# Three weight chunks over GpSimd's queue behind a head's sums, and twenty extra matmuls in five slots

## The chip, the cores and the metric

The kernel runs on one core of a Trainium2 chip. The metric is the time of one execution on the device in microseconds (us); for the kernel before it is the median of three runs. The core's engines are named as in the profile: PE (TensorE, matrix products), DVE (VectorE), ACT (ScalarE), POOL (GpSimd) and SP (SyncE, which here only issues DMA transfers).

## The reference

Three stages follow each other: causal attention with a bias from cumulated `s`, 4 batches of 8 heads, 576 positions, 64 numbers per head; a layer with a clipped gate; a second layer with another gate. The weights `w_in` and `w_out` are float64.

```python
scores = scale * np.matmul(q, k.transpose(0, 1, 3, 2))
cum = np.cumsum(np.maximum(s, 0.0), axis=-1)
bias = -(cum[:, :, :, None] - cum[:, :, None, :])
scores = np.where(causal, -1000000000.0, scores + np.minimum(bias, 0.0))
attn = np.exp(scores - np.max(scores, axis=-1, keepdims=True))
attn = attn / (np.sum(attn, axis=-1, keepdims=True) + 1e-09)
x = np.matmul(attn, v)               # then (2304 tokens, 512)
h = x @ w_in                         # w_in 512 x 2048
x = (h * np.clip(h + 3.0, 0.0, 6.0) / 6.0) @ w_out
h = x @ w2_in
x = (h * (1.0 / (1.0 + np.exp(-h)))) @ w2_out
```

## The kernel before, in words

Attention works on heads of blocks. A block is one batch's first 256 queries (part A) or its other 320 (part B); the blocks come as A0 A1 A2 B0 A3 B1 B2 B3, with eight heads each. The first 22 heads are "whole": their products run in plain fp32. A head of part A goes through PE scores `ps0A`, `ps1A` (line L518), DVE masking into `pb0A`, `pb1A` (L540), ACT's exponential with row sums (L558), DVE's reciprocal of the sums (L567), PE transposes `pt0A` (L586), PE products with v into `poA` (L693), and DVE's scaling into `xtA` (L700), which PE transposes into `pxA` for each pair of heads (L711).

Layer 1 works on finished blocks, and its matmuls lie between those of the heads to come. A step takes one or two of 16 slices of the hidden layer for one block: 24 matmuls into `ph` (L266 to L268), the gate on ACT and DVE (`g`, L279, and `gl`, L286), and 24 matmuls into `acc` (L305 to L307), three for each product since numbers are split in a high and a low part. There is one `ph` bank, so a step's first matmul waits for the gate of the step before. A step of the first kind needs the `wi` and `wo` pieces of its slices.

The weights arrive as 32 chunks, `rawi_0`, `rawo_0`, `rawi_1` and so on, each a load of 512 KB (L147) of float64 words that are turned into two fp32 parts on the chip: ACT takes fields out of the words (L159, L160), POOL scales them (L162), DVE joins them (L178, L182), ACT rounds the high part (L120) and DVE takes the rest as the low part `wi` or `wo` (L193). A `Feed` hands these pieces out in ticks: a tick loads a chunk, takes the fields of the one three ticks before, joins that of four before, and rounds that of five before.

The work is written in slots. A slot scores head `cur`, transposes and multiplies head `p1` (the one before), finishes `p2`, asks for the loads of a head to come, may do a layer-1 step (`mm`), and runs the ticks `tk`. Nine slots have no step, 68 have one each. Three chunks load before slot 0. Slots 0 to 8 tick 0.4 times each, so three ticks fire there: `rawo_1` in slot 2 (`p1` is head 1), `rawi_2` in slot 5 (head 4) and `rawo_2` in slot 7 (head 6); from slot 9 on there are two ticks per slot. Slots without a step run three small bf16 matmuls, `keep_clock` (L86), into the unused `ph` bank. All loads go through SP's queue, where a whole head has four: q, k, v and two rows of cumulated biases, from `pairs` for the first four heads and from `pair_d` in DRAM for the others (L429).

The order of the written program isn't the final one: the kernel passes through a tile scheduler, which sets each engine's order from its own estimate of when things are ready. All engines and queues then work in order.

Of the kernel before, what the change touches and what calls it, by code (L numbers as in the profile page):

```python
# [11 lines left out]
I32 = mybir.dt.int32  # L12
# [5 lines left out]
P = 128  # L18
# [4 lines left out]
def f32(ap):  # L23
    return ap.bitcast(F32)
# [3 lines left out]
def kernel(  # L28
# [15 lines left out]
    nc = tc.nc  # L44

    B, H, D, S = qT.shape
# [36 lines left out]
    def keep_clock(n, beside):  # L83
        for _ in range(n):
            o = idle[:, : beside.shape[-1]]
            nc.tensor.matmul(o, busy[:, :P], beside, start=True, stop=True)  # L86

    def heads_of(x):
        return x.bitcast(BF16).rearrange("p (n two) -> p n two", two=2)[:, :, 1]
# [40 lines left out]
    class Chunk:  # L130
# [7 lines left out]
            pool, tag = self.home  # L138
            return pool.tile(shape, dt, tag=tag, name=f"{name}{self.nm}")

        def load(self):
            if self.src.dtype == F32:
                self.val = self.place([P, DM], F32, "raw")
                nc.sync.dma_start(self.val, self.src)
            else:
                raw = self.place([P, 2 * DM], I32, "raw")
                nc.sync.dma_start(raw, self.src.bitcast(I32))  # L147
                words = raw.rearrange("p (n two) -> p n two", two=2)
                self.words = words[:, :, 0], words[:, :, 1]

# [44 lines left out]
    class Feed:  # L195


        def __init__(self, keys, hi_eng, lo_eng):
            self.ch = [Chunk(*k) for k in keys]
            self.hi_eng, self.lo_eng = hi_eng, lo_eng  # L200
            self.t = 0

        def done(self):
            return self.t >= len(self.ch) + 3 + 2

        def tick(self):
            n = len(self.ch)
            t = self.t - 3
            lo = self.lo_eng[t % len(self.lo_eng)] if 0 <= t - 2 < n else ""
            if lo:  # L210
                self.ch[t - 2].high(self.hi_eng[t % len(self.hi_eng)])
            if 0 <= t < n:
                self.ch[t].fields()
            if lo == "p":
                self.ch[t - 2].low(lo)
            if 0 <= t - 1 < n:
                self.ch[t - 1].join()
            if lo == "v":
                self.ch[t - 2].low(lo)
            if self.t < n:  # L220
                self.ch[self.t].load()
            self.t += 1


# [112 lines left out]
    def bank(kind, shape, name):  # L337
        pool, tag = turns[kind][turn[kind] % len(turns[kind])]
        turn[kind] += 1
        return pool.tile(shape, F32, tag=tag, name=name)  # L340
# [35 lines left out]
    class Head:  # L376
# [3 lines left out]
        def __init__(self, b, part, h, whole, at):  # L380
            self.b, self.part, self.h, self.whole, self.at = b, part, h, whole, at
            self.slot = at % 2
            self.bh = b * H + h
            self.nm = f"{part}{b}_{h}"
            self.chunks = [c for c in range(NCH) if (CH[c][0] < T1) == (part == "A")]
            self.q0 = CH[self.chunks[0]][0]
            self.nk = CH[self.chunks[-1]][0] + CH[self.chunks[-1]][1]
            self.nq = self.nk - self.q0
            self.nkc = self.chunks[-1] + 1
            self.groups = [[0, 1]] if part == "A" else [[0, 1], [2, 3]]  # L390
            self.prob, self.PT, self.pt, self.pS, self.rest = {}, {}, {}, {}, []
            self.pieces = []
            self.odd = h % 2
            for c in self.chunks[:: -1 if self.odd and part == "B" else 1]:
                w = CH[c][0] + CH[c][1]
                self.pieces += [(c, 0, w, True)] if w <= 512 else [
                    (c, 0, w // 2, False), (c, w // 2, w, True)]
            self.full = [c for c in self.chunks if c < NFULL]
# [251 lines left out]
        def av(self):  # L650
# [31 lines left out]
            nc.scalar.copy(tmp[mine, :], po[other, :])  # L682
            self.rest = [(x[mine, :], po[mine, a:z], tmp[mine, a:z]) for x, a, z in outs]

        def av_whole(self):

            b, h, nq = self.b, self.h, self.nq
            n, nch = P, len(self.chunks)
            po = bank("o", [P, nch, D], f"po{self.nm}")
            for c in self.chunks:  # L690
                for kc in range(c + 1):
                    a = CH[c][0] - max(CH[kc][0], self.q0)
                    nc.tensor.matmul(  # L693
                        po[:, c, :], self.PT[kc][0][:, a : a + n], self.va[:, kc, :],
                        start=kc == 0, stop=kc == c,
                    )
            if h % 2 == 0:
                xt[b] = apool.tile([P, nch, 2 * D], F32, tag=f"xZ{h // 2 % 2 + 2}", name=f"xt{self.nm}")
            r = self.sums[:, : nch].rearrange("p (c o) -> p c o", o=1)
            nc.vector.tensor_tensor(  # L700
                out=xt[b][:, :, h % 2 * D :][:, :, :D], in0=po,
                in1=r.to_broadcast([P, nch, D]), op=ALU.mult,
            )
# [89 lines left out]
    def slot(cur, p1, p2, nx, loads, mm, tk=(0, 0, 0, 0)):  # L793

        nonlocal step
        ng = len(p1.groups) if p1 else 0
        npc = len(cur.pieces) if cur else 0

        def scores(i):
            if i < npc:  # L800
                cur.score(i)
                cur.soft(i)

        def exps(i):
            if i < npc:
                cur.expo(i)

        def transposed(i):
            if i < ng:
                p1.trans(i)  # L810
                p1.trans_low(i)

        scores(0)
        scores(1)
        exps(0)
        if p2:
            p2.av_sum()
        ticks(tk[0])
        if mm:
            first(step, 0)  # L820
        if p1:
            p1.v_high()
        exps(1)
        scores(2)
        if nx:
            nx.qk_high()
        transposed(0)
        if p1 and p1.part == "B" and p1.odd:
            p1.tail_parts(p1.raw[:, :NFULL, :], p1.raw[:TAIL, NFULL, :])
        if p1 and not mm:  # L830
            keep_clock(3, heads_of(p1.prob[1]))
        if p1:
            p1.v_low()
        exps(2)
        if cur:
            cur.load_v()
        if nx and npc <= 3:
            nx.qk_low()
        ticks(tk[1])
        if mm:  # L840
            first(step, 1)
            gate_high(step)
        scores(3)
        if nx and npc > 3:
            nx.qk_low()
        exps(3)
        for hd in loads:
            hd.load()
        transposed(1)
        if cur:  # L850
            cur.norm()
        ticks(tk[2])
        if mm:
            second(step - 1, 0)
        if mm:
            gate_low(step)
        if p1 and p1.part == "B" and not p1.odd:
            p1.tail(cur)
        ticks(tk[3])
        if nx:  # L860
            nx.places()
        for hd in loads:
            hd.load_cum()
        if mm:
            second(step - 1, 1)
        if p1:
            p1.av()
        if mm:
            step += 1
# [17 lines left out]
    for has_head, has_step in plan:  # L887
        cur = at(k) if has_head else None
        nx = at(k + 1) if has_head else None
        loads = []  # L890
        while has_head and loaded < len(heads) and loaded <= k + (
            2
        ):
            loads.append(heads[loaded])
            loaded += 1
        k += has_head and cur is not None
        tk = [0, 0, 0, 0]
        if not feed.done():
            rate = ((0.4,)*9+(2,))[min(nslot, len(((0.4,)*9+(2,))) - 1)]
            for i in range(4):  # L900
                feed_at += rate / 4
                tk[i] = int(feed_at)
                feed_at -= tk[i]
        slot(cur, p1, p2, nx, loads, has_step, tk)
        if nslot == 9:
            split_rows()
        p1, p2 = cur, p1
        nslot += 1
        if nslot == H + 1:
            p2.av_sum()  # L910
            p2 = None
            split1(0)
            turns["s"] = turns["s"][:1]
        if has_step and step in first_step[1:NB1]:
            blk = first_step.index(step)
            assert k - (cur is not None) >= (blk + 1) * H
            if p2:
                p2.av_sum()
                p2 = None
            if blk == NB1 - 1:  # L920
                cx.close()
                xpool = cx.enter_context(
                    tc.tile_pool(name="xlast", bufs=1, side="right", reuse_waits="tile")
                )
            split1(blk)
            if blk == NB1 - 1:
                break
# [364 lines left out]
```

## Time and profile before

| | |
|---|---|
| median of 3 runs | 996.71 us (996.62 to 997.44) |
| the profiled execution | 997.93 us |
| its span, first to last instruction | 996.1 us |
| mean granted clock of PE | 0.992 |
| busy: PE, DVE, ACT, POOL | 973.4, 737.3, 510.8, 266.4 us |
| transfers | 125.41 MB, 126 GB/s over the span |

The span is read in stretches of time, each with the busy time of every engine, the clock granted to PE (1.00 is 2.4 GHz, half of it 1.2 GHz) and the share of the DMA engines. An engine that is full in a stretch bounds it; where none is, the waits tell which engine waited for which. Timelines list instructions in order of start; matmuls overlap, so the pitch from start to start is what one costs, not its duration.

### The profile page before, as it was taken

How to read it: one execution, taken by the hardware profiler on the slowest of the kernel's cores; microseconds unless marked ns; L12 is line 12 of the kernel's file. 1: busy time of each engine (PE TensorE's matmuls, PEld its weight loads, DVE VectorE, ACT ScalarE, POOL GpSimd, SP SyncE). 2: the span in 40 equal slices, each digit the busy share in tenths (PEclk: the TensorE clock that was granted, in tenths of full speed). 3: DMA queues.
4: the chain of work that ended last, by engine and by line, in shares of the span. 5: the costliest groups of instructions: out<-in, count | busy, mean ns of one | idle time of the engine just before them, and what ended most of it. 6: DMA issues, size and time to landing. Idle time of an engine off the chain costs nothing.

```text
span 996.1 us, 17938 instructions
## 1 busy us (share of the span) xinstructions
PE 973.4 (98%) x6268; PEld 896.2 (90%) x6268; DVE 737.3 (74%) x1757; ACT 510.8 (51%) x1177; POOL 266.4 (27%) x323
## 2 busy tenths in 40 slices
PE   8998999999999999999999999999999999999997
PEld 5888999999999999999997877898988989889996
DVE  6899998888789888988866899779674434743343
ACT  6898645555455555555546566455443323432332
POOL 2122433343333443433425466425000000000000
PEclk9899999999999999999999999999999999999999
DMA  5885122312222223222215967434354233442421
GB/s 176 238 285 187 41 55 76 90 49 60 83 77 75 72 59 92 60 61 83 60 32 180 394 225 239 163 116 190 135 193 169 81 141 116 162 154 75 148 75 64
DMA packets 54419, 125.41 MB, mean 126 GB/s; under 512 B 12332, under 2 KB 34076, under 8 KB 51000
## 3 DMA queue, kind: packets, MB, share of 16 engines
q1 hardware_dynamic: 53880, 123.60, 37.7%
q8 instruction: 50, 0.82, 0.3%
q10 hardware_dynamic: 448, 0.66, 0.2%
q14 instruction: 41, 0.34, 0.1%
HBM read 99.52 MB, written 24.69 MB: 125 GB/s over the span
## 4 chain that ended last, share of the span: by engine, by line
PE 74%; DVE 12%; DMA 4%; issue 4%; POOL 3%; ACT 1%; SPq 1%; POOLq 0%; DVEq 0%; ACTq 0%
PE a L1089 6%; PE a L1090 6%; PE a L1091 6%; PE h L1072 5%; PE h L1074 5%; PE h L1073 5%; PE ph L266 5%; PE ph L267 4%; PE ph L268 4%; PE acc L306 4%; PE acc L305 4%; PE acc L307 4%; PE poB L678 3%; DMA rawi<-in_w2i_dram 2%; POOL rawi L167 2%
## 5 line engine op out<-in xcount | busy, mean ns | idle before, releaser
L266 PE MATMUL ph<-xh,wi 128*128 128x256 f32 (+1 forms) x512 | 153.7, 302 | 4.4 <-DVE g L279 4.2
L306 PE MATMUL acc<-gl,wo 128*128 128x256 f32 (+1 forms) x512 | 151.6, 298 | 1.6 <-DVE gl L286 1.6
L267 PE MATMUL ph<-xl,wi 128*128 128x256 f32 (+1 forms) x512 | 151.4, 296 | 0.0
L268 PE MATMUL ph<-xh,wi 128*128 128x256 f32 (+1 forms) x512 | 151.2, 295 | 0.0
L307 PE MATMUL acc<-gh,wo 128*128 128x256 f32 (+1 forms) x512 | 150.3, 295 | 0.0
L305 PE MATMUL acc<-gh,wo 128*128 128x256 f32 (+1 forms) x512 | 143.6, 297 | 0.0
L1131 ACT ACTIVATE gh<-h 128x384 fp32r<-128x384 f32 x96 | 50.3, 524 | 178.7 <-DVE h L1139 178.5
L1089 PE MATMUL a<-wo,gh 128*128 128x512 f32 x288 | 113.6, 395 | 1.5 <-ACT gh L1131 1.1
L1090 PE MATMUL a<-wo,gh 128*128 128x512 f32 x288 | 113.1, 393 | 0.0
L266 PEld LDWEIGHTS ph<-xh,wi 128*128 128x128 f32 x512 | 96.9, 189 | 9.6 <-PE acc L307 1.9
L306 PEld LDWEIGHTS acc<-gl,wo 128*128 128x128 f32 x512 | 96.6, 189 | 5.7 <-DVE gl L286 2.7
L267 PEld LDWEIGHTS ph<-xl,wi 128*128 128x128 f32 x512 | 97.1, 190 | 3.1
L268 PEld LDWEIGHTS ph<-xh,wi 128*128 128x128 f32 x512 | 96.9, 189 | 3.0
L307 PEld LDWEIGHTS acc<-gh,wo 128*128 128x128 f32 x512 | 96.6, 189 | 3.3
L305 PEld LDWEIGHTS acc<-gh,wo 128*128 128x128 f32 x512 | 95.4, 188 | 3.5 <-DVE gh L122 0.2
L1091 PE MATMUL a<-wo,gl 128*128 128x512 f32 x288 | 90.5, 393 | 0.0
L1133 DVE TENSOR_TENSOR gl<-h,gh 128x384 fp32r<-128x384 f32 x96 | 53.4, 556 | 40.4 <-ACT h L1132 38.8
L114 POOL TENSOR_SCALAR gh<-g 128x512 fp32r<-128x512 f32 x68 | 50.0, 738 | 102.7 <-DVE g L279 88.2
L1139 DVE TENSOR_TENSOR h<-h,u 128x384 f32<-128x384 f32 x72 | 40.0, 556 | 49.8 <-PE h L1074 49.4
L1072 PE MATMUL h<-x0t,w 128*128 128x384 f32 x192 | 65.0, 339 | 0.7 <-DVE u L1139 0.7
L1073 PE MATMUL h<-x1t,w 128*128 128x384 f32 x192 | 65.0, 338 | 0.0
L1074 PE MATMUL h<-x0t,w 128*128 128x384 f32 x192 | 64.8, 338 | 0.0
(222 smaller groups left out, 2526.6 us busy)
## 6 DMA issues: line engine op xcount, KB each, us to landing
w<-w_d SPq DMA_DIRECT2D x18, 1792.0 KB
w_d<-w SPq DMA_DIRECT2D x8, 1792.0 KB
k2B<-in_kT_dram SPq DMA_DIRECT2D x64, 144.0 KB
rawi<-in_w1i_dram SPq DMA_DIRECT2D x16, 512.0 KB
rawo<-in_w1o_dram SPq DMA_DIRECT2D x16, 512.0 KB
rawi<-in_w2i_dram SPq DMA_DIRECT2D x16, 512.0 KB
rawo<-in_w2o_dram SPq DMA_DIRECT2D x16, 512.0 KB
q2B<-in_qT_dram SPq DMA_DIRECT2D x64, 80.0 KB
```

The lines of the kernel that those rows point to most:

```text
L266: nc.tensor.matmul(o, wih[:, cs], xh[c], start=c == 0, stop=False)
L267: nc.tensor.matmul(o, wih[:, cs], xl[c], start=False, stop=False)
L268: nc.tensor.matmul(o, wil[:, cs], xh[c], start=False, stop=c == NDC - 1)
L305: nc.tensor.matmul(a, woh[:, cs], gh[:, jj, :], start=b0, stop=False)
L306: nc.tensor.matmul(a, woh[:, cs], gl[:, jj, :], start=False, stop=False)
L307: nc.tensor.matmul(a, wol[:, cs], gh[:, jj, :], start=False, stop=b1)
L1072: nc.tensor.matmul(ps, w[:, 0, cs], xh[:, c, :], start=c == 0, stop=False)
L1073: nc.tensor.matmul(ps, w[:, 0, cs], xl[:, c, :], start=False, stop=False)
L1074: nc.tensor.matmul(ps, w[:, 1, cs], xh[:, c, :], start=False, stop=c == 1)
L1089: nc.tensor.matmul(accs[t], gh[:, k, cs], woh, start=b0, stop=False)
L1090: nc.tensor.matmul(accs[t], gh[:, k, cs], wol, start=False, stop=False)
L1091: nc.tensor.matmul(accs[t], gl[:, k, cs], woh, start=False, stop=b1)
```

## The change

Three things are written differently. In slots 0 to 8 a chunk's load is issued by POOL instead of SP, and POOL first copies two numbers of the sums of head `p1` into the chunk's buffer, so the load waits for that head's reciprocal and, as POOL works in order, for what stands ahead of it on POOL. `beside(4)` puts four extra matmuls, of the high halves of `ident` with those of the head's second probability tile, 128x256 in bf16, into the head's `po` bank, which the real products overwrite later; that is in the five slots 9 to 13, the first with a step, where `p1` is heads 8 to 12 (A1_0 to A1_4). They stand after the head's transposes. And `po` is taken from the pool at that point rather than at the products.

```diff
-        def load(self):
+        def load(self, behind=None):
+            queue = nc.sync if behind is None else nc.gpsimd
...
                 raw = self.place([P, 2 * DM], I32, "raw")
-                nc.sync.dma_start(raw, self.src.bitcast(I32))
+                if behind is not None:
+                    pool_copy(f32(raw[:1, : behind.shape[-1]]), behind)
+                queue.dma_start(raw, self.src.bitcast(I32))
...
             if self.t < n:
-                self.ch[self.t].load()
+                self.ch[self.t].load(self.behind)
...
+        def place_out(self):
+            self.po = bank("o", [P, 512], f"po{self.nm}")
+            return self.po
+
+        def beside(self, n):
+            x = heads_of(self.prob[1])
+            o = self.place_out()[:, : x.shape[-1]]
+            for _ in range(n):
+                nc.tensor.matmul(o, heads_of(ident), x, start=True, stop=True)
...
-            po = bank("o", [P, nch, D], f"po{self.nm}")
+            po = (self.po or self.place_out())[:, : nch * D].rearrange("p (c d) -> p c d", d=D)
...
         if p1 and not mm:
             keep_clock(3, heads_of(p1.prob[1]))
+        if p1 and mm and nslot < H + 1 + 5:
+            p1.beside(4)
...
+        feed.behind = p1.sums[:1, :2] if p1 and nslot <= H else None
         slot(cur, p1, p2, nx, loads, has_step, tk)
```

The line numbers move by 3 to 15: L147, L162, L178, L193, L279 and L711 become L150, L165, L181, L196, L283 and L726, and the extra matmuls are L698.

The scheduler gives a new order on all engines, not only at these places. Three of them follow, with the buffer's number behind each name.

On POOL, the conversions of the second to the fourth pair of chunks, in slots 0 to 9, before:

```order
L162 TENSOR_SCALAR rawi_1_175<-rawi_1_175 128x512
L162 TENSOR_SCALAR rawo_1_261<-rawo_1_261 128x512
L162 TENSOR_SCALAR rawi_2_360<-rawi_2_360 128x512
L162 TENSOR_SCALAR rawo_2_457<-rawo_2_457 128x512
L162 TENSOR_SCALAR rawi_3_538<-rawi_3_538 128x512
```

and with the change, where L114 is the copy from a head's sums (`sums_129` is head 1's, `sums_127` head 4's, `sums_131` head 6's):

```order
L165 TENSOR_SCALAR rawi_1_175<-rawi_1_175 128x512
L114 TENSOR_SCALAR rawo_1_261<-sums_129 1x2
L150 DMA rawo_1_261<-in_w1o_dram 128x1024
L114 TENSOR_SCALAR rawi_2_361<-sums_127 1x2
L150 DMA rawi_2_361<-in_w1i_dram 128x1024
L165 TENSOR_SCALAR rawo_1_261<-rawo_1_261 128x512
L165 TENSOR_SCALAR rawi_2_361<-rawi_2_361 128x512
L114 TENSOR_SCALAR rawo_2_459<-sums_131 1x2
L150 DMA rawo_2_459<-in_w1o_dram 128x1024
L165 TENSOR_SCALAR rawo_2_459<-rawo_2_459 128x512
L165 TENSOR_SCALAR rawi_3_541<-rawi_3_541 128x512
```

Each of the three loads now stands on POOL behind its copy, and the conversion of the first (`rawo_1`, L165) behind the copy and the load of the second.

On DVE, the last conversions (L182, L193) and the gate of step 13 (`g_1884`) before:

```order
L193 TENSOR_TENSOR wo_14_1962<-mago_14_1836,wo_14_1962 128x512
L480 TENSOR_TENSOR vsA_6_1984<-vaA_6_1868,vsA_6_1984 128x2x64
L178 SCALAR_TENSOR_TENSOR mago_15_1964<-mago_15_1964,rawo_15_1777 128x512
L567 RECIPROCAL sums_133<-sums_133 128x2
L182 ISA magi_15_1902<-rawi_15_1711,magi_15_1902 128x1024
L122 COPY xA_2_1960<-pxA_5_1957 128x256
L279 SCALAR_TENSOR_TENSOR g_1884<-g_1884,ph_1843 128x512
L624 TENSOR_TENSOR tlA_6_1997<-pt0A_6_1992,thA_6_1996 128x384
L540 ISA pb2B_0_2054,mxB_0_2051<-ps0B_0_2080,cmask 128x384
```

The next rows hold the three last conversions: `mago_15` (L182), `wi_15` and `wo_15` (L193), up to ten rows behind that gate. With the change, around the gate of step 12 (`g_1777`; L196 is what L193 was, L283 what L279 was):

```order
L470 TENSOR_TENSOR kaB_0_1951<-k2B_0_1914,khB_0_2011 64x576
L122 CAST vsA_6_2007<-vaA_6_1891 128x2x64
L196 TENSOR_TENSOR wo_15_2113<-mago_15_1987,wo_15_2113 128x512
L469 TENSOR_TENSOR qsB_0_2010<-q2B_0_1913,qsB_0_2010 64x320
L571 TENSOR_SCALAR sums_133<-sums_133 128x2
L122 COPY xA_2_1983<-pxA_5_1980 128x256
L485 TENSOR_TENSOR vsA_6_2007<-vaA_6_1891,vsA_6_2007 128x2x64
L283 SCALAR_TENSOR_TENSOR g_1777<-g_1777,ph_1736 128x512
L629 TENSOR_TENSOR tlA_6_2020<-pt0A_6_2015,thA_6_2019 128x384
L572 RECIPROCAL sums_133<-sums_133 128x2
```

All 32 chunks are now converted ahead of the gate of step 12; before, three conversions came after the gate of step 13. The gate of step 8 has 24 chunks ahead of it, where it had 20. From the gate of step 14 on the orders are the same.

On PE, the start of slot 9, before:

```order
L693 MATMUL poA_7_496<-inA_7_372,thA_7_481 128x64 x3
L711 MATMUL pxA_7_501<-ident,xtA_6_467 128x128 x2
L586 MATMUL pt0A_0_548<-ident,pb0A_0_460 128x128
L586 MATMUL pt0A_0_548<-ident,pb1A_0_461 128x128 x2
L586 MATMUL pt0A_1_634<-ident,pb0A_1_493 128x128
L586 MATMUL pt0A_1_634<-ident,pb1A_1_494 128x128 x2
L518 MATMUL ps0A_3_693<-inA_3_566 128x128
L518 MATMUL ps1A_3_696<-inA_3_566 128x256
```

and with the change:

```order
L708 MATMUL poA_7_499<-inA_7_374,thA_7_484 128x64 x3
L523 MATMUL ps0A_3_704<-inA_3_574 128x128
L523 MATMUL ps1A_3_707<-inA_3_574 128x256
L726 MATMUL pxA_7_504<-ident,xtA_6_470 128x128 x2
L591 MATMUL pt0A_0_551<-ident,pb0A_0_463 128x128
L591 MATMUL pt0A_0_551<-ident,pb1A_0_464 128x128 x2
L698 LDWEIGHTS ident
L698 MATMUL poA_0_557<-pb1A_0_464,ident 128x256
```

The extra matmuls of head A1_0 (L698) stand behind `pxA_7` and the head's first transposes (three more like the last follow), and the scores of head A1_3 have moved ahead of these.

## Rows read from the trace of the kernel before

**Rows 1.** Table by stretches: us, busy (x instructions) PE PEld DVE ACT POOL, PEclk, DMA share, GB/s.
```profile
15.00:20.00 5.00, 3.88 (x30) 2.94 (x30) 4.86 (x24) 4.68 (x17) 0.00 (x0) 1.00 0.57 173
20.00:28.00 8.00, 8.00 (x38) 7.22 (x38) 5.15 (x22) 5.01 (x15) 0.65 (x1) 0.57 0.59 156
28.00:41.00 13.00, 10.98 (x85) 9.72 (x84) 10.38 (x44) 11.16 (x34) 1.59 (x3) 0.99 0.80 232
41.00:48.00 7.00, 7.00 (x32) 6.82 (x33) 6.49 (x17) 5.97 (x15) 2.18 (x3) 0.52 1.00 277
48.00:85.00 37.00, 33.90 (x266) 31.77 (x264) 36.97 (x109) 35.61 (x87) 8.43 (x11) 1.00 0.89 289
85.00:95.00 10.00, 7.81 (x60) 7.06 (x61) 8.54 (x25) 8.77 (x22) 2.76 (x5) 1.00 0.50 171
95.00:132.00 37.00, 35.14 (x292) 34.03 (x292) 36.81 (x79) 22.71 (x51) 15.21 (x20) 1.00 0.16 43
132.00:600.00 468.00, 466.69 (x3523) 445.88 (x3522) 397.23 (x1039) 253.18 (x628) 186.28 (x241) 1.00 0.32 100
```

**Rows 2.** Waits of PE, 48 to 132 us: total us, times, longest.
```profile
PE ph L266 <- DVE g L279: 3.9, 5, 1.3
```

**Rows 3.** Groups on DVE by shape, 20 to 132 us: busy us, mean ns.
```profile
L178 DVE SCALAR_TENSOR_TENSOR magi<-magi,rawi 128x512 int32<-128x512 int32 x14 | 10.7, 767 | 0.6 <-POOL rawi L162 0.6
...
L193 DVE TENSOR_TENSOR wi<-magi,wi 128x512 fp32r<-128x512 f32 x14 | 9.9, 710 | 1.0 <-ACT wi L120 0.8
```

**Rows 4.** Timeline of PE: start us, duration us, [idle before <-releaser].
```profile
19.06 0.50 PE L86 MATMUL idle<-pb1A,busy 128*128 128x256 bf16 x3 [0.65 <-ACT pb1A L558]
```

**Rows 5.** Timeline of SP's DMA issues, 15 to 32 us.
```profile
16.15 0.43 SPq L147 DMA_DIRECT2D rawo<-in_w1o_dram  x1
16.63 0.29 SPq L429 DMA_DIRECT2D inA<-pair_d  x1
...
21.20 0.34 SPq L147 DMA_DIRECT2D rawi<-in_w1i_dram  x1
...
28.29 0.43 SPq L147 DMA_DIRECT2D rawo<-in_w1o_dram  x1
```

**Rows 6.** Who waited for line L147's loads, 0 to 140 us: us, times.
```profile
  PEld ps0A L518: 0.6, 1
```

**Rows 7.** Timeline of PE, 39 to 41.2 us.
```profile
39.82 0.44 PE L711 MATMUL pxA<-ident,xtA 128*128 128x128 f32 x2 [1.16 <-DVE xtA L700]
```

**Rows 8.** Timeline of DVE, 15 to 32 us: reciprocals of heads 1, 4 and 6.
```profile
19.03 0.15 DVE L567 RECIPROCAL sums<-sums 128x2 f32<-128x2 f32 x1
...
24.85 0.16 DVE L567 RECIPROCAL sums<-sums 128x2 f32<-128x2 f32 x1
...
30.43 0.16 DVE L567 RECIPROCAL sums<-sums 128x2 f32<-128x2 f32 x1
```

**Rows 9.** Timeline of POOL, 15 to 34 us.
```profile
29.47 0.66 POOL L162 TENSOR_SCALAR rawi<-rawi 128x512 f32<-128x512 f32 x1 [7.70 <-ACT magi L160]
```

**Rows 10.** Timeline of ACT, 19.5 to 29 us.
```profile
19.81 0.68 ACT L159 ACTIVATE rawo<-rawo 128x512 int32<-128x512 uint32 x1
...
20.95 0.39 ACT L558 ACTIVATE pb0A<-pb0A,mxA 128x128 f32<-128x128 f32 x1
...
28.18 0.66 ACT L159 ACTIVATE rawi<-rawi 128x512 int32<-128x512 uint32 x1
```

**Rows 11.** Timeline of PE, 30.3 to 31.2 us.
```profile
30.44 0.51 PE L86 MATMUL idle<-pb1A,busy 128*128 128x256 bf16 x3
30.79 0.27 PE L586 MATMUL pt0A<-ident,pb0A 128*128 128x128 f32 x1
```

**Rows 12.** Timeline of DVE, 131 to 132.4 us: gate of step 13.
```profile
131.34 0.68 DVE L279 SCALAR_TENSOR_TENSOR g<-g,ph 128x512 f32<-128x512 f32 x1
```

**Rows 13.** Timeline of PE, 131 to 132.6 us.
```profile
131.24 0.28 PE L307 MATMUL acc<-gh,wo 128*128 128x256 f32 x1
...
131.58 0.28 PE L307 MATMUL acc<-gh,wo 128*128 128x256 f32 x1
```

More of the change, by code (lines that the diff above doesn't have):

```diff
@@ L139, in place @@
             return pool.tile(shape, dt, tag=tag, name=f"{name}{self.nm}")
-        def load(self):
+        def load(self, behind=None):
+            queue = nc.sync if behind is None else nc.gpsimd
             if self.src.dtype == F32:
                 self.val = self.place([P, DM], F32, "raw")
-                nc.sync.dma_start(self.val, self.src)
+                queue.dma_start(self.val, self.src)
             else:
                 raw = self.place([P, 2 * DM], I32, "raw")
-                nc.sync.dma_start(raw, self.src.bitcast(I32))
+                if behind is not None:
+                    pool_copy(f32(raw[:1, : behind.shape[-1]]), behind)
+                queue.dma_start(raw, self.src.bitcast(I32))
                 words = raw.rearrange("p (n two) -> p n two", two=2)
@@ L201, in __init__ @@
             self.t = 0
+            self.behind = None
         def done(self):
@@ L391, in __init__ @@
             self.prob, self.PT, self.pt, self.pS, self.rest = {}, {}, {}, {}, []
+            self.po = None
             self.pieces = []
```

## Prediction

> **What bounds the kernel now.** I read the table by stretches first, then the orders of the engines, then the timelines around two gaps. The table [rows 1] has TensorE (PE) full from 132 us on (466.69 of 468), so a microsecond lost or won earlier reaches the end as PE work left over at 132 us. From 48 to 132 us VectorE (DVE) is full: it is idle 0.03 us in 48 to 85, 1.46 in 85 to 95 and 0.19 in 95 to 132, while PE is idle 3.10 + 2.19 + 1.86 = 7.15 us. There PE waits for DVE: the largest such wait is that of a layer-1 step's first matmul (`ph`) for the gate of the step before, 3.9 us in five waits [rows 2]. Between the gates DVE converts weight chunks, three operations of 0.71 to 0.77 us each per chunk [rows 3].
>
> Before 48 us the same table shows the clock: 0.57 in 20 to 28 us and 0.52 in 41 to 48, with PE full; the two levels are 1.2 and 2.4 GHz. What that costs is 8 x 0.43 + 7 x 0.48 = 3.4 + 3.4 = 6.8 us of PE work. Ahead of each stands a stretch in which PE was partly idle. Ahead of the first, PE waits 0.65 us for ScalarE's (ACT) exponential, up to 19.06 us [rows 4], and for loads: a chunk's transfer is issued at 16.15 us and head 4's two rows (`pair_d`) right behind it on the same SP queue [rows 5]; 0.6 us of waiting by head 4's first score is put down to that chunk's issue line [rows 6]. Ahead of the second, PE waits 1.16 us for DVE's `xtA` [rows 7]; DVE has chunk work in front of it. DVE too is idle while PE is slow: 2.85 us in 20 to 28, 2.62 in 28 to 41, 0.51 in 41 to 48 [rows 1], with 0.14 before 20: 7.8 us in all up to 132 us.
>
> **The change, part by part.** *Three chunks move to GpSimd's (POOL) queue.* SP loses three issues, 0.34 to 0.43 us each, and the head loads behind move up by that; this is 1.2 us of SP, which only matters where a load is late, and I count it inside the term x below. On POOL each load stands behind a one-row copy from a head's sums, so it can't be issued before that head's reciprocal: 19.03 instead of 16.15 us, 24.85 instead of 21.20, 30.43 instead of 28.29 [rows 5, 8]. POOL works in order: the conversion of the first of the three now stands behind the copy that waits for 24.85 (the order on POOL above). POOL had nothing else to do then; it stood idle 7.70 us before its next conversion [rows 9]. Head 4's rows no longer queue behind the chunk. That may take away the wait at 19.8 us, though not ACT's 0.65 at 19.06.
>
> From issue to first use the old load took 19.81 - 16.15 = 3.66 us [rows 5, 10]. By the same time the new ones land at 22.7, 28.5 and 34.1 us. No row of before has a load on POOL, so I bound its lateness by 0 and by the waits that can be seen: the exponential stands behind such a chunk's first conversion on ACT, 1.14 us from 19.81 to 20.95 [rows 10]. I take 0, because the DVE order puts the first chunk's conversion 15 rows later than it was, and the two others where they were. The Trainium skill speaks against it: by "SBUF — State Buffer", section "SBUF: two separate sides", a load that GpSimd issues has its descriptors written by GpSimd, which is shut out of a shared port while VectorE runs certain operations, and one that takes 620 ns alone took 3100 there. By that rule each of the three would be some 2.5 us later still (an estimate from that page); no run here shows it yet.
>
> *Twenty more matmuls* of 128x256 bf16, four in each of five slots. The same kind stands in the slots without a step: three started at 30.44 us and the next work at 30.79 [rows 11], 0.117 us each, so 2.3 us in all, at half clock twice that, 4.7. They lie in 41 to 95 us, where PE is idle for at least 3.10 + 2.19 us anyway, beside work that waits for DVE, so I count 0; the bounds are 0 and 4.7. Can they keep the clock up in 41 to 48? The PE order shows the first four behind `pxA` of head 7 and the transposes of slot 9, and so behind the 1.16 us gap, which comes ahead of the fall. What has moved ahead of that gap is one head's scores, which may fill a part of it. I expect the two to shorten that stretch at best; this too is inside x.
>
> *The new order.* This is what the diff doesn't show, and what I think decides. The scheduler has put chunk conversions earlier against the gates on DVE. At the gate of step 8, 24 chunks are done where it was 20; at the gate of step 12, all 32, where it was 28 (11 operations more); from the gate of step 14 on the two orders agree. The piece of order above shows it: before, the gate of step 13 (`g_1884`) stands ahead of the last three conversions; now `wo_15`, the very last, stands ahead of the gate of step 12 (`g_1777`). So at the new gate 12 DVE has done what it had done at the old gate 13, with three conversions more, and without two operations of step 13's gate (`g` and `gl`): one operation more, +0.6 us. The old gate 13 stood at 131.34 us [rows 12], and PE then went on with step 14; now PE goes on with step 13. It is behind by one step, 24 `ph` and 24 `acc` matmuls and 3 transposes. Three matmuls took 131.58 - 131.24 = 0.34 us [rows 13], so, with the transposes counted like these, 51 x 0.113 = 5.8 us. After it PE is full, so this is not caught up: 0.6 + 5.8 = **+6.4 us**, if DVE is as full up to that gate as it was.
>
> From this goes **x**, the DVE idle time that the change removes before that point, bounded by 7.8, all there is in the table, and on the other side by a loss of 1.1, one hold-up of ACT by a late chunk (the 1.14 us above). The idle time of 20 to 48 us comes to 6.0; about half of it hangs on the first stretch and on the late loads, which the change touches, the other half on the second gap, which stays ahead of the added matmuls. So half, 3.0, and a third of the 1.46 in 85 to 95, 0.5: x = 3.5. The 6.8 us of clock aren't subtracted as well: they are PE time, and PE has 7.15 us to spare until 132 us.
>
> **Sum.** +6.4 - 3.5 + 0 = +2.9 us. The profiled execution took 997.93 us (a span of 996.1 and 1.8 around it), so it becomes 1000.8; the median of the three runs, 996.71, is 1.2 lower, which gives **999.6 us**. For x from -1.1 to 7.8 this case alone would run from 995.3 to 1004.2. A measurement of this kernel tells about 0.2%, 2 us, from no change.
>
> **Rivals.**
> *The gain and the shift cancel.* If x is 5 or more (the first stretch gone and the second short), the sum is -1.4 to +1.4: about 997. For it: all of the idle DVE time up to 48 us lies in or next to those two stretches. Against it: the gap at 39 us comes from DVE's own order.
> *Faster.* Both half-clock stretches go, and the moved conversions don't bind, because DVE starts its full stretch earlier by all the time that PE gains, and the operations that stand earlier only fill idle time. Then -6.8 and the 2.3 us of matmuls: -4.5, 992.2 us; with one stretch and part of the other, down to -2. For it: PE is 98% busy, and no other bound is left. Against it: DVE is idle 0.03 us in 48 to 85.
> *Slower by more, through the in-order queues.* The load on POOL lands late, ACT and DVE stand at that chunk's conversion with the exponential or a head's `pb` behind it, x is 0, and PE's new gap brings a third half-clock stretch (3.4): +9.8, 1006.5 us. It decides from the point at which the second of the three chunks is used later than 28.2 us on ACT by over 1 us. For it: 28.5 us by my own sum is already on the edge. Against it: POOL is free. The page's rule on descriptors would lead here.
> *The change doesn't do what it says:* the gap at 19 us stays, since ACT's exponential makes it and not the chunk; x is then about 1, +5.4. I leave it inside the first case.
>
> **How the numbers follow.** The forecast with its upper part has 0.40, the cancelling one 0.28, the faster one 0.22, the in-order one 0.10. So faster 0.22, same 0.28, slower 0.50. The range goes from 993.2, which takes in most of the faster case (0.08 lies below), to 1004.2, the upper end of the first case; the 0.10 of the last rival lies above.
>
> **What would show it.** In the table by stretches of the changed kernel: the clock in 20 to 28 us back near 1.0 if head 4's rows come earlier, and a second stretch after slot 9 that is still there; DVE without idle time from about 45 us to the gate of step 12, and that gate near 128 to 131 us, where PE starts on step 13 rather than 14; PE full after it. The forecast is wrong if DVE shows idle time ahead of the gates of steps 8 to 12 (then the order costs nothing), if both stretches are at full clock, or if the three loads show up late in the waits of ACT or DVE.

## The result and the profile after

| | before | with the change |
|---|---|---|
| median | 996.66 us (4 runs, 995.23 to 997.44) | 1009.81 us (4 runs, 1007.30 to 1010.39) |
| the profiled execution, its span | 997.93, 996.1 us | 1010.39, 1008.6 us |
| PE busy, PE idle in the span | 973.4, 22.7 us | 981.3, 27.3 us |
| mean granted clock | 0.992 | 0.984 |

The ratio is 1.0123, with a 95% interval from 1.0088 to 1.0158: slower by some 13 us, where the forecast was 999.6 us in a range of 993.2 to 1004.2. Seen from PE, the span is 12.5 us longer by 7.9 us of busy time and 4.6 of idle time.

The table by stretches of the changed kernel, columns as in [rows 1]:

```profile
15.00:20.00 5.00, 4.53 (x35) 3.46 (x32) 5.00 (x28) 4.75 (x18) 0.48 (x2) 1.00 0.34 92
20.00:28.00 8.00, 5.68 (x40) 4.81 (x38) 4.46 (x18) 5.03 (x16) 1.84 (x4) 0.91 0.75 211
28.00:41.00 13.00, 10.08 (x57) 8.66 (x56) 8.13 (x32) 7.70 (x24) 2.73 (x4) 0.76 0.68 200
41.00:48.00 7.00, 6.96 (x30) 6.32 (x31) 5.85 (x20) 6.22 (x17) 1.31 (x2) 0.50 0.91 283
48.00:60.00 12.00, 12.00 (x64) 11.25 (x63) 9.34 (x28) 9.79 (x22) 2.56 (x3) 0.62 0.64 199
60.00:85.00 25.00, 22.82 (x184) 21.43 (x183) 24.38 (x70) 23.28 (x57) 6.99 (x7) 1.00 0.86 316
85.00:95.00 10.00, 5.64 (x41) 4.79 (x39) 9.46 (x23) 8.07 (x19) 2.83 (x4) 0.99 0.67 184
95.00:110.00 15.00, 13.15 (x83) 12.54 (x84) 10.75 (x30) 10.71 (x27) 3.11 (x4) 0.78 0.11 30
110.00:132.00 22.00, 21.06 (x177) 20.44 (x176) 21.88 (x53) 14.17 (x32) 7.97 (x11) 1.00 0.16 45
132.00:600.00 468.00, 466.69 (x3581) 448.55 (x3581) 394.03 (x1045) 249.70 (x629) 182.48 (x244) 1.00 0.31 97
```

Compare it with [rows 1]. From 132 to 600 us PE is as full as it was: 466.69 of 468 us in both. Ahead of that, the half clock lasts longer: 0.76 in 28 to 41 us, 0.50 in 41 to 48, 0.62 in 48 to 60 and 0.78 in 95 to 110; counted over whole stretches, as in the prediction, that is 0.7 + 3.1 + 3.5 + 4.6 + 3.3 = 15.2 us of PE time, where it was 6.8; since PE was also idle for a part of them, this is an upper bound. And DVE is idle: 3.54 + 4.87 + 1.15 + 2.66 us from 20 to 60, and 4.25 in 95 to 110; 17.8 us from 15 to 132, where it was 7.8.

POOL's timeline of the changed kernel shows the held loads (copy L114, then load L150):

```profile
19.17 0.18 POOL L114 TENSOR_SCALAR rawo<-sums 1x2 f32<-1x2 f32 x1 [5.25 <-DVE sums L572]
19.70 0.75 POOL L150 DMA_DIRECT2D rawo<-in_w1o_dram  x1 [0.35 <-POOL rawo L114]
21.32 0.18 POOL L114 TENSOR_SCALAR rawi<-sums 1x2 f32<-1x2 f32 x1 [0.88 <-DVE sums L572]
21.81 0.58 POOL L150 DMA_DIRECT2D rawi<-in_w1i_dram  x1 [0.31 <-POOL rawi L114]
...
31.25 0.48 POOL L114 TENSOR_SCALAR rawo<-sums 1x2 f32<-1x2 f32 x1 [1.67 <-ACT thA L120]
32.02 0.58 POOL L150 DMA_DIRECT2D rawo<-in_w1o_dram  x1 [0.30 <-POOL rawo L114]
```

They are issued at 19.70, 21.81 and 32.02 us. The view of the load line gives their time from issue to landing:

```profile
DMA to landing us min/median/max: 5.3/5.3/6.5
```

So 5.3 to 6.5 us. Before, the first of them was in use 3.66 us after its issue, and ACT did not wait for it. ACT's timeline shows who stands at them:

```profile
24.98 0.65 ACT L162 ACTIVATE rawo<-rawo 128x512 int32<-128x512 uint32 x1 [1.98 <-DMA rawo<-in_w1o_dram]
...
26.08 0.46 ACT L120 COPY thA<-pt0A 128x384 f32<-128x384 f32 x1
...
38.55 0.65 ACT L162 ACTIVATE rawo<-rawo 128x512 int32<-128x512 uint32 x1 [3.29 <-DMA rawo<-in_w1o_dram]
...
40.54 0.45 ACT L120 COPY thA<-pt0A 128x384 f32<-128x384 f32 x1
```

ACT waits 1.98 us for the first load and 3.29 for the third, and the copy `thA`, which PE needs for a head's products, stands behind them on ACT, from 26.08 and from 40.54 us. PE's timeline shows the two gaps that this makes:

```profile
26.59 1.54 PE L708 MATMUL poA<-inA,thA 128*128 128x64 f32 x6 [2.13 <-ACT thA L120]
...
41.04 1.54 PE L708 MATMUL poA<-inA,thA 128*128 128x64 f32 x6 [2.90 <-ACT thA L120]
```

2.13 and 2.90 us, and the clock is at 0.50 right after each (0.50 in 28 to 32 us and in 42 to 56). The extra matmuls of slot 9 ran at 46.90 us, inside the second stretch.

A third gap comes at 92 us. SP's timeline and PE's row:

```profile
87.20 0.36 SPq L150 DMA_DIRECT2D rawi<-in_w1i_dram  x1
87.60 1.56 SPq L150 DMA_DIRECT2D rawo<-in_w1o_dram  x1
89.26 0.37 SPq L450 DMA_DIRECT2D vaA<-in_v_dram  x1
```

```profile
95.36 1.51 PE L708 MATMUL poA<-vaA,thA 128*128 128x64 f32 x6 [3.46 <-DMA vaA<-in_v_dram]
```

Two chunk loads of 512 KB were issued on SP just ahead of a load of a head's v, and PE waited 3.46 us for that v; the clock was at 0.50 from 95 to 101 us.

### The profile page after: what moved, and what is told of

The parts are those of the page before. It is cut to its first block, busy times and chain, and to the rows that moved or that the text cites. A ratio compares the mean times of both kernels' runs of the same rounds, so it can differ in the third digit from the quotient of the medians.

```text
span 1008.6 us, 18002 instructions
## 1 busy us (share of the span) xinstructions
PE 981.3 (97%) x6288; PEld 903.8 (90%) x6288; DVE 736.7 (73%) x1757; ACT 511.5 (51%) x1177; POOL 269.1 (27%) x329
## 4 chain that ended last, share of the span: by engine, by line
PE 75%; DVE 9%; DMA 7%; issue 2%; ACT 2%; POOL 2%; SPq 1%; POOLq 0%; DVEq 0%; ACTq 0%
PE a L1107 6%; PE a L1108 6%; PE a L1109 6%; PE h L1090 5%; PE h L1091 5%; PE h L1092 5%; PE ph L270 5%; PE ph L271 5%; PE ph L272 5%; PE acc L310 4%; PE acc L311 4%; PE acc L309 4%; PE poB L683 3%; DMA rawi<-in_w2i_dram 2%; DMA rawo<-in_w1o_dram 2%
## 5 line engine op out<-in xcount | busy, mean ns | idle before, releaser
L114 POOL TENSOR_SCALAR gh<-g 128x512 fp32r<-128x512 f32 x68 | 48.3, 713 | 95.5 <-DVE g L283 88.2
```

## The experiments

The theory after this: two terms add up at the gate of step 12, from which on PE has the last word. One is DVE's idle time ahead of it, from late loads and the clock that falls behind their gaps. The other is the DVE work that the new order puts ahead of it, some 7 us. Rivals: lateness alone; the order alone; the extra matmuls or the earlier place of the `po` bank. DVE's idle and busy time from the start to the gate of step 12 can be read in one row for each kernel: start:end, length, busy (instructions), then the clock and the DMA columns. Before and with the change:

```profile
0.00:123.33 123.33, 108.26 (x314) 0.94 0.61 187
```

```profile
0.00:140.02 140.02, 115.07 (x329) 0.89 0.52 166
```

Work 108.26 and 115.07 us: +6.8. Idle 123.33 - 108.26 = 15.1 and 140.02 - 115.07 = 25.0 us: +9.9. Together the two are, by the way they are counted, the delay of that gate; what the runs can show is whether the whole time follows it, and whether one of the two is enough for a loss.

All experiments start from the changed kernel. The medians of the kernel before beside them were 997.26 us (e1 to e4), 996.48 (e5 to e8) and 997.75 (e9 to e12); its single runs spread from 994.3 to 1006.5 us.

**e1: the loads without the matmuls.**

```diff
-        if p1 and mm and nslot < H + 1 + 5:
-            p1.beside(4)
```

> The three loads on POOL behind the sums, without the twenty extra matmuls. If the loads make the loss (late landing, engines that stand at them in order, half clock after it), this is within 2 us of the whole change, 1008 to 1012 us, with PE gaps of over 2 us at about 25 and 38 us again. If the extra matmuls or the place of their po bank made it, it falls to within 3 us of the kernel before, 994 to 1000.

1008.22 us, ratio 1.0107 (1.0087 to 1.0126). The loads make nearly all of it. The waits of ACT from 15 to 60 us and of PE from 15 to 130 (total, times, longest):

```profile
ACT rawo L162 <- DMA rawo<-in_w1o_dram: 6.3, 2, 4.9
```

```profile
PE poA L708 <- ACT thA L120: 7.2, 4, 4.7
```

ACT waited 6.3 us for two loads and PE 7.2 us for `thA`. The gap of the third load was larger than in the change (4.7 us), and that of the first shrank (1.6 us).

**e2: the matmuls without the loads.**

```diff
-        feed.behind = p1.sums[:1, :2] if p1 and nslot <= H else None
+        feed.behind = None
```

> The twenty matmuls alone, all chunks on SP as before; the number of conversions ahead of each gate is then within 2 to 7 operations of the kernel before, not 12 as in the change. If the loads make the loss: 995 to 999 us. If the matmuls do: over 1003. If they shorten the half-clock stretch at 41 to 48 us as they could: under 995.

996.06 us, ratio 0.9987 (0.9976 to 0.9999). So the matmuls and the earlier bank cost nothing that can be measured. In the table by stretches of e2 the clock is no longer halved in 41 to 48 us (it was 0.52):

```profile
41.00:48.00 7.00, 5.59 (x42) 4.82 (x42) 6.66 (x20) 6.30 (x15) 2.35 (x3) 1.00 0.84 251
```

PE got that stretch back, and the time hardly moved: step 14 started at 132.1 us, as before.

**e3: the same hold, but ACT's queue** (without the matmuls, as in e4 to e7 and in e9 and e10).

```diff
-            queue = nc.sync if behind is None else nc.gpsimd
+            queue = nc.sync if behind is None else nc.scalar
```

> The three loads held behind the same sums, but issued by ACT, without the extra matmuls. The order on DVE is then nearly that of the kernel before (21 conversions ahead of the first gate, 64 ahead of that of step 8; 21 and 62 before, 25 and 74 in the change). If POOL's queue is what lands them late: the load takes under 4.5 us from issue to first use, the gaps at 25 and 38 us shrink below 1 us, and the time is 994 to 1000. If the holding itself makes them late, or ACT's waiting for the copy costs as much: 1003 or more.

1004.24 us, ratio 1.0056 (1.0030 to 1.0082). ACT's timeline:

```profile
19.81 0.41 ACTq L150 DMA_DIRECT2D rawo<-in_w1o_dram  x1
...
24.94 0.67 ACT L162 ACTIVATE rawo<-rawo 128x512 int32<-128x512 uint32 x1 [1.00 <-DMA rawo<-in_w1o_dram]
...
29.39 0.33 ACTq L150 DMA_DIRECT2D rawo<-in_w1o_dram  x1
...
33.91 0.68 ACT L162 ACTIVATE rawo<-rawo 128x512 int32<-128x512 uint32 x1 [1.15 <-DMA rawo<-in_w1o_dram]
```

Where ACT waited for them, the loads took 5.1 and 4.5 us to their first use. The gaps became small (0.9 us at most on PE from 15 to 48 us) and the clock was whole until 41 us, but the time did not come back to 1000: partly a miss. The row to the gate of step 12, +3.2 us of work and 16.8 - 15.1 = +1.7 of idle time, has the rest:

```profile
0.00:128.32 128.32, 111.50 (x330) 0.97 0.60 184
```

**e4: POOL's queue without the hold.**

```diff
-                if behind is not None:
-                    pool_copy(f32(raw[:1, : behind.shape[-1]]), behind)
```

> The three loads on POOL without the copy, so they are issued early; no extra matmuls. The order on DVE is moved further than in the change (35 conversions ahead of the first gate where it was 25, and 78 ahead of that of step 8). If lateness makes the loss, the gaps at 25 and 38 us go and the time is 995 to 1002. If the order of conversions makes it, the loss stays or grows: 1008 to 1016.

1008.40 us, ratio 1.0110 (1.0088 to 1.0131). The loads were issued from 3.4 to 4.6 us. This is mostly the order: +7.2 us of work, and only 17.8 - 15.1 = +2.7 of idle time.

```profile
0.00:133.25 133.25, 115.49 (x329) 0.90 0.55 175
```

The gain of early loads was also spent in another place. The DMA engines were full from 6 to 12 us (share 1.03), and PE waited 4.4 us for one input, a wait that the profile puts down to a chunk's load (columns as in [rows 1], then PE's row):

```profile
6.00:12.00 6.00, 4.26 (x20) 1.76 (x18) 0.42 (x1) 1.35 (x2) 0.29 (x1) 1.00 1.03 391
```

```profile
14.64 0.77 PE L521 MATMUL ps0A<-inA 66*128 66x128 f32 x2 [4.39 <-DMA rawi<-in_w1i_dram]
```

**e5: only the third load on POOL.**

```diff
-        feed.behind = p1.sums[:1, :2] if p1 and nslot <= H else None
+        feed.behind = p1.sums[:1, :2] if p1 and 7 <= nslot <= H else None
```

> Only the third load (rawo_2) goes over POOL behind the sums, without the extra matmuls; the first two stay on SP. The order on DVE is near that of before (64 conversions ahead of the gate of step 8, 62 before, 74 in the change). If a late load by itself makes the loss: ACT waits 3 to 5 us for it at 34 to 39 us, PE has a gap of over 2 us there and half clock after it, step 1 starts 4 to 8 us later than before (46.0), and the time is 1000 to 1004. If the order of conversions does it: 996 to 999.

1003.04 us, ratio 1.0064 (1.0041 to 1.0086). This is lateness almost alone. ACT's and PE's rows, and DVE's:

```profile
37.83 0.65 ACT L162 ACTIVATE rawo<-rawo 128x512 int32<-128x512 uint32 x1 [3.31 <-DMA rawo<-in_w1o_dram]
```

```profile
39.44 0.88 PE L708 MATMUL poA<-inA,thA 128*128 128x64 f32 x6 [3.03 <-ACT thA L120]
```

```profile
0.00:128.10 128.10, 108.64 (x312) 0.91 0.56 179
```

ACT waits 3.31 us, PE 3.03 for `thA`; the work is +0.4 us and the idle time 19.5 - 15.1 = +4.4. Step 1 started at 49.2 us, 3.2 later than before and so below the 4 to 8 that were expected.

**e6: only the first two.** As e5, with `nslot < 7`.

> The first two loads go over POOL behind the sums, the third stays on SP. Ahead of the gate of step 8 there are 65 conversions (62 before, 74 in the change). If the third load's lateness is the main part: step 1 starts within 3 us of before (46.0), and the time is 996 to 1000. If any load on POOL is as costly: step 1 at 50 or later, and 1002 to 1008.

1005.69 us, ratio 1.0093 (1.0073 to 1.0114), step 1 at 54.6 us. That the third load is the main part falls. The work, +7.5 us, is not conversions here: 85 of them stand ahead of the gate of step 12, where it was 87, so other operations came ahead of it. And the second load was late, with `pb1A`'s exponential behind it on ACT, and PE's `keep_clock` waited for that (ACT's row, PE's row):

```profile
28.04 0.65 ACT L162 ACTIVATE rawi<-rawi 128x512 int32<-128x512 uint32 x1 [1.99 <-DMA rawi<-in_w1i_dram]
```

```profile
29.78 0.80 PE L86 MATMUL idle<-pb1A,busy 128*128 128x256 bf16 x3 [1.94 <-ACT pb1A L563]
```

**e7: only the second.** As e5, with `4 <= nslot < 7`.

> Only the second load (rawi_2) goes over POOL. By the traces so far this one hardly waited (0.3 to 0.8 us on ACT), but the order on DVE is moved nearly as far as in the change: 73 conversions ahead of the gate of step 8, 62 ahead of that of step 7. If the order is a cost of its own, step 1 starts within 2 us of before, the stretch from the start of step 8 to that of step 9 takes 12 to 15 us where it took 8.8, and the time is 1000 to 1004. If only lateness counts: 996 to 998.

1005.41 us, ratio 1.0081 (1.0065 to 1.0096). ACT did not wait for this load at all (it landed in 4.2 us). Idle time to the gate of step 12 is 16.0 - 15.1 = +0.9 us, work is +5.4:

```profile
0.00:129.62 129.62, 113.62 (x320) 0.91 0.55 177
```

Step 8 started at 88.67 us and step 9 at 100.51; the 11.8 us between are a little under the 12 to 15 expected, step 1 was 3.3 us late rather than 2, and the time is 1.4 above the range expected. This is the order as a cost of its own, for one load that was never late: the clock was at 0.50 in 41 to 48 us and 0.73 in 48 to 60 here too, but DVE was busy 12.00 of 12 us in 48 to 60.

**e8: matmuls in slot 9 alone.** As e2, with `nslot < H + 1 + 1`.

> The extra matmuls in slot 9 alone (four of the twenty), all loads on SP, the order on DVE as before. If the half clock at 41 to 48 us is paid for by DVE anyway (PE is idle 7 us until 132 us), this is 995.5 to 997.5 whether or not the clock is kept; if the clock is the bound, it gains the 3.4 us: 993 to 994.5.

998.31 us, ratio 1.0019 (1.0001 to 1.0037): no gain, though the clock was whole in 41 to 48 us with four matmuls and the order that came with them:

```profile
41.00:48.00 7.00, 5.45 (x42) 4.88 (x41) 6.27 (x18) 6.38 (x16) 2.87 (x3) 1.00 0.92 289
```

**e9: the hold on SP's own queue.**

```diff
-            queue = nc.sync if behind is None else nc.gpsimd
+            queue = nc.sync
```

> The same three loads held behind the same sums, but left on SP's queue; no extra matmuls. On DVE this order has 83 conversions ahead of the gate of step 12, where before has 87 and the change 96. If the delay at that gate is DVE's idle time ahead of it plus the work put ahead of it, the work term is -2.6 us (4 operations of 0.65) and the rest is idle time: 994 to 998 if the head loads behind the held ones are not late, 1000 or more if they are, with DVE idle 5 us more ahead of that gate. If lateness alone counted, the fewer conversions would give nothing back and it would be 997 or more in any case.

1001.50 us, ratio 1.0056 (1.0029 to 1.0083). The heads' loads were late. PE's waits from 15 to 130 us (total, times, longest):

```profile
PE ps0A L523 <- DMA k2A<-in_kT_dram: 3.9, 1, 3.9
PE poA L708 <- DMA vaA<-in_v_dram: 2.5, 1, 2.5
PE ps0A L523 <- DMA inA<-pair_d: 2.2, 1, 2.2
```

The wait of 2.2 us ended at 25.83 us, among the held loads. The two longer ones did not: they ended at 75.07 and 89.18, and the last held load was issued at 29.67, so that SP stood at the held loads does not explain them. The first held load took 4.2 us to its first use, which waited for it (SP's and ACT's rows):

```profile
19.30 0.34 SPq L150 DMA_DIRECT2D rawo<-in_w1o_dram  x1
```

```profile
23.48 0.65 ACT L162 ACTIVATE rawo<-rawo 128x512 int32<-128x512 uint32 x1 [0.86 <-DMA rawo<-in_w1o_dram]
```

Idle time to the gate of step 12 was 133.28 - 109.41 - 15.1 = +8.8 us. The work was +1.1, not the -2.6 of the count of conversions: 323 instructions of DVE came ahead of that gate, where it was 314, so the count of conversions alone doesn't give the work.

**e10: POOL, held one head earlier.**

```diff
-        feed.behind = p1.sums[:1, :2] if p1 and nslot <= H else None
+        feed.behind = p2.sums[:1, :2] if p2 and nslot <= H else None
```

> The three loads on POOL, held behind the sums of the head before (p2 in place of p1), so issued about one slot earlier; no extra matmuls. 93 conversions stand ahead of the gate of step 12 (87 before): +3.9 us of work. If the loads come early enough, ACT waits under 1.5 us for them, DVE's idle time ahead of that gate is within 2 us of before, and the time is 999 to 1003. If a load on POOL is late wherever it is held: 1004 to 1008.

1007.08 us, ratio 1.0081 (1.0052 to 1.0110): the second case. Only the third load came much earlier (issued at 23.34 us), and ACT then waited 0.5 us for it; the first still made the same gap on PE. The work was +5.4 us where the count of conversions gave +3.9. Its loads' landing and PE's row:

```profile
DMA to landing us min/median/max: 5.4/6.0/6.2
```

```profile
26.59 1.54 PE L708 MATMUL poA<-inA,thA 128*128 128x64 f32 x6 [2.17 <-ACT thA L120]
```

**e11 and e12: e2 again, and two matmuls in place of four.**

> The kernel of the second run once more, for its difference from before alone: 994.5 to 997.5 us, a ratio between 0.997 and 1.000 if the small gain was real.

> Two extra matmuls in place of four in each of the five slots, all loads on SP; the order on DVE is that of before to within one operation. If what the matmuls give is the clock at 41 to 48 us, and DVE holds PE up until 132 us all the same: 995.5 to 997.5. If the clock were the bound: 993 to 994.5.

998.25 us, ratio 1.0008 (0.9985 to 1.0031), and 997.89, ratio 0.9994 (0.9972 to 1.0016). The small gain of e2 did not come again, and no version here beats the kernel before clear of its noise. In e11's profile both stretches that had been at half clock are whole, and the gate of step 12 stands at 123.34 us, where it was 123.33:

```profile
20.00:28.00 8.00, 6.54 (x51) 5.74 (x51) 6.15 (x26) 6.84 (x21) 1.30 (x2) 1.00 0.54 150
41.00:48.00 7.00, 5.89 (x45) 5.33 (x46) 6.66 (x18) 6.15 (x16) 2.93 (x3) 1.00 0.95 293
```

The two terms for all, from the profiled executions (us; differences from before):

| | idle to gate 12 | work to gate 12 | sum | span |
|---|---|---|---|---|
| the change | +9.9 | +6.8 | +16.7 | +12.5 |
| e1 loads only | +4.5 | +7.2 | +11.7 | +10.6 |
| e3 ACT's queue | +1.7 | +3.2 | +5.0 | +4.9 |
| e4 POOL, no hold | +2.7 | +7.2 | +9.9 | +9.3 |
| e5 third | +4.4 | +0.4 | +4.8 | +8.8 |
| e6 first two | +3.8 | +7.5 | +11.2 | +11.7 |
| e7 second | +0.9 | +5.4 | +6.3 | +8.2 |
| e9 hold on SP | +8.8 | +1.1 | +10.0 | +9.2 |
| e10 one head earlier | +4.3 | +5.4 | +9.7 | +9.3 |
| e2 matmuls only | +0.8 | -0.5 | +0.3 | -1.3 |
| e8 one slot | -0.4 | -1.3 | -1.6 | +0.2 |
| e11, as e2 | +0.8 | -0.8 | 0.0 | -1.9 |
| e12 two each | +0.4 | -1.9 | -1.5 | -1.3 |

The profiled executions of e5, e6 and e9 took 1006.70, 1009.56 and 1007.07 us, 3.7 to 5.6 above the medians of these runs, so their rows show more loss than a median execution has. In most rows the sum gives the span's difference to within 2 us. In the change it is 4.2 too high, and in e5 4.0 too low. A part lies in PE's idle time behind that gate: 9.76 us in the change and 13.79 in e5, where it was 10.98 before. The rest was not found.

## Why the prediction was right or wrong

*What bounds the kernel before: right.* DVE decides up to 132 us and PE after it. The sharpest sign is e8: the clock in 41 to 48 us went from 0.52 to 1.00, which would be 3.4 us if PE were the bound, for four more matmuls, and the time did not fall (the ratio's interval starts at 1.0001). e2 and e11 have the clock back as well, but their twenty matmuls, 2.3 us by the prediction's price, could hide most of a gain. In e8 the gate of step 12 came 1.6 us earlier, so a part of the clock may arrive there. That the 6.8 us of clock must not be subtracted as well was right, and the faster rival, which took all of it, did not come.

*The new order: right in kind, and near in size.* The step said 11 operations more ahead of the gate of step 12. The traces have 9, 96 conversions where it was 87, with 5.1 us more of busy time; all of DVE's work there grew by 6.8. e4 and e7 show this term with little lateness beside it, at 1008.4 and 1005.4 us. By the prediction's own working, with the gate where it came: 140.02 - 131.34 = 8.7, and 5.8 for one step of PE work, are 14.5 us; 12.5 were measured. Where the other 2.0 went was not found.

*The landing of the loads: this step failed.* "I take 0, because the DVE order puts the first chunk's conversion 15 rows later than it was, and the two others where they were." Two things were wrong in it. The 3.66 us of the old load, for which nothing had waited, were no measure for the new ones, which took 5.3 to 6.5. And the order that mattered was ACT's, not DVE's: the chunk's first conversion stands there ahead of a head's `thA`. The bound of one hold-up, 1.14 us, was the length of the chunk's work on ACT and not of the wait for it; the waits were 1.98 and 3.29.

*x: wrong in sign, and this is the miss.* "So half, 3.0, and a third of the 1.46 in 85 to 95, 0.5: x = 3.5." DVE's idle time up to the gate of step 12 grew by 9.9 us, so x was -9.9. It grew right behind the two gaps (20 to 60 us: 12.2 us where it was 6.0), and by 4.2 us in 95 to 110, behind the wait for a head's v. How much of this the gaps make and how much the half clock behind them, no run separates. The wait for v was not foreseen at all: the prediction counted SP's three missing issues as help, and did not read where the other chunk loads stood on SP against the heads' loads.

*The first stretch.* 20 to 28 us did come back, to 0.91, as the step hoped, but e11 has 1.00 there with all loads on SP, so the moved loads are not shown to be the reason; the next gap, at 24.5 us, took the place of the one at 19.

*The matmuls: right.* They cost nothing that can be measured (e2, e11). With them alone the clock was whole in 41 to 48 us (e2, e8, e11), which is more than was expected of them; in the change they run when it has already fallen.

*The rival that came.* "Slower by more, through the in-order queues" was priced at 1006.5 us with x at 0 and a third half-clock stretch. It named the mechanism, but its turning point was on the wrong chunk: the second was used at 27.23 us, in time, and the first and the third were late. It had a chance of 0.10. Its two parts should not have been a rival but the middle of the range: e1, e3 to e7, e9 and e10 all show more work ahead of the gate, or idle time, or both, with the second or the third load alone on POOL and with the hold on each of three queues.

What stays open: how much of the late landing is POOL's own. On ACT's queue the loads took 4.5 and 5.1 us under the same hold, on SP's 4.2 (e9); chunk loads on SP for which ACT waited, without a hold, took 4.4 (e7) and 4.5 (e5); on POOL they took 4.2 (e7) to 7.5 (e4). The Trainium skill's "SBUF — State Buffer", section "SBUF: two separate sides", has a load issued by GpSimd that took 620 ns alone and 3100 beside a VectorE copy; as an estimate from that page, each would be some 2.5 us later. No run here shows that this is the reason: what VectorE ran beside the loads was not varied, and e4's loads landed from 8 us on, while VectorE was busy 0.42 of the 6 us from 6 to 12 and the DMA engines were full.

## What to carry to other kernels

When a load moves, look on every engine that uses it for what stands behind its first use, and price the wait with a landing time from the busiest stretch, not from one old load that happened to be in time. Where a scheduler sets the order, compare how much work stands ahead of a late gate before and after, on the engine that is full there: it grew by 6.8 us, though nothing in the diff told it. Count all operations: the count of one kind alone was off by 3.7 us in e9 and missed all of it in e6. A clock that is won back on an engine which then waits for another is worth nothing.

## What was not expected of the hardware

The issue of a load of 512 KB took 0.55 to 0.76 us of POOL's time, where SP's issues of the same size mostly took 0.33 to 0.43, and such loads on POOL took 4.2 to 7.5 us to land, over the change, e1, e4 to e7 and e10. With four bf16 matmuls in one slot (e8) the clock was whole over the stretch that had been at 0.52; what else the new order changed there was not taken apart.
